# Half of z loaded as bf16 behind v, denser early score pairs, w2 turned by one DMA transpose, and the last output tiles sent one by one

## The chip, the cores and the metric

The kernel runs on one core of one Trainium2 chip. The metric is the device time of one execution in microseconds. "Span" is the profiled execution's time from its first to its last instruction, 2.4 us less than the device time in the kernel before. A time is compared with runs of the kernel before on the same chip, because the chips differ a little.

## The reference

Attention without softmax, gated by u, then a maxout feed-forward layer (8 batches, 3072 rows, 256 columns, z 64 wide, hidden size 1024):

```python
scores = (1.0 / S) * np.matmul(z, z.transpose(0, 2, 1))
attn = np.maximum(scores, 0.0) ** 2
x = (u * np.matmul(attn, v)).reshape(B * S, D)
g = np.maximum(x @ w1, x @ w2)          # computed as relu(x(w1 - w2)) + x w2
out = g @ w_out
```

## The kernel before

The scores are symmetric, so each batch computes only the blocks on and above the diagonal and gets the others by turning them with DMA transposes ("mirrors", tile at_sb). A batch has six groups of 512 rows. Group i runs 48 steps; a step is a pair of matmuls that share the array, one on each half of the rows. Score pairs (two matmuls, two evictions with relu, one square) are made ahead of need, at chosen steps ("slots"), across batch borders. The score matmuls of a batch read zT, the turned z. For batch 0 the opening makes it on TensorE; for batch 1 and later one DMA transpose does it. All DMA transposes and all output stores are issued from the SP queue, in program order; loads that cast from float32 to bf16 are issued from GpSimd's queue.

Names of tiles in the profile lines below: s_ps holds scores as the matmuls leave them in PSUM (the memory that TensorE writes), r_sb the scores after relu, a_sb the squared scores, at_sb their mirrors, zd the doubled z that is turned into zT, acc the sums of a group in PSUM, h_sb these sums after the "drain" (their copy out of PSUM), and un and uT are u before and after its turn.

The parts that matter here (cuts marked by `# ...`):

```python
def pair_slots(i):                       # i counts groups over all batches
    if i == 0: return [1, 3] + list(range(6, 40, 4))
    if i == 1: return list(range(3, 41, 4))
    # ...
V_LATE = [(3, 14), (4, 8), (4, 14), (5, 2), (5, 8), (5, 14)]   # v of batch 1: (group, step)

def ahead(upto):                         # score pairs; some have one half evicted on VectorE
    early = done < 22
    score_pair(*pairs[done], dve_half=1 if early and done % 3 == 0 else None, halves=done == 0)
# ...
# opening: SP loads z of batch 0 in float32 in three pieces (4, 8, 12 tiles); GpSimd's queue
# loads v, then u; GpSimd copies the third piece twice to bf16 (zd); TensorE turns zd into zT
for slot, (n, dc) in enumerate(steps_of(i)):
    ahead(...)                           # emits mirrors too, as blocks become complete
    attn_unit(...)
    # ...
    if later and n % 4 == 0 and (i > 1 or i == 1 and n > 12):
        mirror(*later.pop(0))            # deferred mirrors of groups 0 and 1
    if i == 2 and n == 16:               # w15 = w1 - w2; w2T by 16 TensorE transposes
        # ...
    if (g, n) == (3, 4):                 # zT of the next batch
        double_z(b + 1, 0, NT)           # two VectorE copies
        zT_dma(b + 1)                    # one DMA transpose, SP queue
# after group 2: W2o = w2 w_out from w2T, then the first feed-forward
```

Of the kernel before, what the change touches and what calls it, by code (L numbers as in the profile page):

```python
# [11 lines left out]
def kernel(  # L12
# [10 lines left out]
    nc = tc.nc  # L23
    fp32 = mybir.dt.float32
# [223 lines left out]
    def ff2(b, g, xT, g_sb, last=False):  # L248
        dst = by_tile(out[ds(b * S, S), :])[:, ds(g * G, G), :]
        o_sb = opool.tile([P, G, D], fp32, name="o_sb")  # L250
        for t0 in range(0, G, 2):
            o_ps = mm_psum.tile([P, 2, D], fp32, name="o_ps", tag="mm")
            for t in range(2):
                for dc in range(KD):
                    nc.tensor.matmul(  # L255
                        o_ps[:, t, :],
                        xT[:, dc, ts(t0 + t, P)],
                        W2o_sb[:, dc, :],
                        start=(dc == 0),
                        stop=False,  # L260
                    )
                for nb in range(KF):
                    nc.tensor.matmul(  # L263
                        o_ps[:, t, :],
                        g_sb[:, nb, ts(t0 + t, P)],
                        w_out_sb[:, nb, :],
                        start=False,
                        stop=(nb == KF - 1),
                    )
            nc.scalar.copy(o_sb[:, t0 : t0 + 2, :], o_ps)  # L270
            if last:
                nc.sync.dma_start(out=dst[:, ds(t0, 2), :], in_=o_sb[:, t0 : t0 + 2, :])
        if not last:
            nc.sync.dma_start(out=dst, in_=o_sb)

# [22 lines left out]

    def pair_slots(i):
        if i == 0:  # L300
            return [1, 3] + list(range(6, 40, 4))
        if i == 1:
            return list(range(3, 41, 4))
        if ff_follows(i):
            return [3, 9, 15, 21, 26, 31, 36, 40]
        return [0, 5, 10, 15, 20, 25, 30, 41]
# [39 lines left out]
    with tc.manual_schedule():  # L346
        z32a = first_z(0, 4)
        z32b = first_z(4, 8)
        z32c = first_z(12, 12)
        warm = consts.tile([P, GW], bf16)  # L350
        nc.vector.memset(warm, 0.0)
        load_v(0, 0, G)
        make_identity(nc, ident)
        for g in range(1, NG):
            load_v(0, g * G, G)
        load_u(0, 0)
        load_u(0, 1)
        w1_sb = tpool.tile([P, KD, Dff], bf16, name="w1", tag="at_sb")
        w2_sb = tpool.tile([P, KD, Dff], bf16, name="w2", tag="at_sb")
        w2T_sb = tpool.tile([P, KD, KF, P], bf16, name="w2T", tag="at_sb")  # L360


        def new_acc():
            return {
                (half, dc): acc_psum.tile([P, GW], fp32, name=f"acc{half}{dc}")
                for half in range(2)
                for dc in range(KD)
            }

        first_acc = new_acc()  # L370

        def keep_warm(cols):
            for w in cols:
                nc.tensor.matmul(
                    first_acc[0, 0][:, :w], warm[:, :P], warm[:, :w], start=True, stop=True
                )

        keep_warm([GW] * 5 + [P] * 2)
        double_first(z32a, 0, 4)
        zT_pe(0, 0, 4, "dve")  # L380
        keep_warm([P] * 5)
        double_first(z32b, 4, 4)
        double_first(z32b, 8, 4, at=4)
        on_pool = (nc.gpsimd.tensor_copy, nc.gpsimd.tensor_copy)
        for c in range(0, 12, 4):
            double_first(z32c, 12 + c, 4, at=c, copies=on_pool)
        ahead(1)
        zT_pe(0, 4, 8, "dve")
        keep_warm([P] * 2)
        ahead(2)  # L390
        keep_warm([P] * 4)

        waiting, sums = [], None
        for i, (b, g) in enumerate(groups):
            acc = new_acc() if i else first_acc
            new, slots = {}, pair_slots(i)
            for slot, (n, dc) in enumerate(steps_of(i)):
                k = need[i, n]
                ahead(max(k, min(done + 1, k + AHEAD)) if slot in slots else k)
                if i == 0 and slot in (10, 22):  # L400
                    zT_pe(0, 12 if slot == 10 else 20, 8 if slot == 10 else 4, "act")
                attn_unit(b, g, tiles_of(b, g)[n], acc, dc, n == 0, n == NT - 1)
                if n == NT - 1 and not ff_follows(i):
                    if i < 2:
                        new[dc] = drain_fast(acc, dc)
                    else:
                        new.update(drain(acc, [dc]))
                if dc:
                    continue
                if i in (1, 2) and n == 10:  # L410
                    for h in sums.values():
                        nc.vector.tensor_add(h[0], h[0], h[1])
                    sums = {k: h[0] for k, h in sums.items()}
                if i and n == 12:
                    waiting.append((*groups[i - 1], gate(*groups[i - 1], sums)))
                if i == 0 and n == 14:
                    turn_u(0, 0)
                if i + 1 < len(groups):
                    if i and n == 1:
                        load_u(*groups[i + 1])  # L420
                    if n == 16:
                        turn_u(*groups[i + 1])
                if (i, n) in ((0, 20), (1, 10)):

                    w_in = ((w2_sb, moe_w2), (w1_sb, moe_w1)) if i == 0 else ((w_out_sb, moe_w_out),)
                    nc.vector.memset(w_in[0][0][:, 0, 0:1], 0.0)
                    for w_sb, w in w_in:
                        nc.gpsimd.dma_start(
                            out=w_sb, in_=w.rearrange("(c p) f -> p c f", p=P)
                        )  # L430
                if later and n % 4 == 0 and (i > 1 or i == 1 and n > 12):
                    later.sort(key=lambda block: block[2])
                    mirror(*later.pop(0))
                if i == 2 and n == 16:
                    nc.vector.tensor_sub(w15_sb, w1_sb, w2_sb)
                    for dc in range(KD):
                        tp = mm_psum.tile([P, KF, P], bf16, name="tpw", tag="mm")
                        for j in range(KF):
                            nc.tensor.transpose(
                                tp[:, j, :], w2_sb[:, dc, ts(j, P)], ident  # L440
                            )
                        nc.scalar.copy(w2T_sb[:, dc, :, :], tp)
                if b + 1 < B:
                    late = int(b == 0)
                    if (g, n) == (2, 10 if b else 20):
                        load_z(b + 1, 0, NT, held=late)
                    if (g, n) == (3, 4):
                        double_z(b + 1, 0, NT)
                        zT_dma(b + 1)
                    if g >= 3 and n in (8, 14) and not late:  # L450
                        load_v(b + 1, V_ORDER[2 * (g - 3) + (n == 14)] * G, G)
                    if late and (g, n) in V_LATE:
                        load_v(1, V_ORDER[V_LATE.index((g, n))] * G, G, held=True)
            if i == 2:
                for dc in range(KD):
                    ps = mm_psum.tile([P, D], fp32, name="w2o_ps", tag="mm")
                    for nb in range(KF):
                        nc.tensor.matmul(
                            ps,
                            w2T_sb[:, dc, nb, :],  # L460
                            w_out_sb[:, nb, :],
                            start=(nb == 0),
                            stop=(nb == KF - 1),
                        )
                    nc.scalar.copy(W2o_sb[:, dc, :], ps)

            now = waiting if ff_follows(i) else []
            g_sbs = [ff(w) for w in now[:1]]
            sums = new or drain(acc, range(KD))
            for j, w in enumerate(now):  # L470
                if j:
                    g_sbs.append(ff(w))
                ff2(*w, g_sbs[j])
            if now:
                waiting = []
        w = (*groups[-1], gate(*groups[-1], sums))
        ff2(*w, ff(w), last=True)
# [29 lines left out]
```

## Time and profile before

968.79 us, median of five runs (968.57 to 969.14). What matters:

| what | number |
|---|---|
| TensorE busy | 954.8 of 966.4 us |
| TensorE waits after 60 us | none over 0.2 us |
| first attention matmul / start of group 1 / start of W2o | 7.32 / 23.00 / 52.03 us |
| zT of batch 1: issued / landed / first needed | 74.02 / 80.4 / 86.80 us |

TensorE is the bound: matmuls fill the span but for the opening and the tail. The view of waits of TensorE for the whole span lists who ended its idle time. A line names the engine and the tile that it was about to write, then, behind the arrow, the engine and tile that it waited for, then us in total, times, longest; one wait of 0.2 us is left out:

```profile
PE acc_134 L374 <- DVE warm L351: 1.2, 1, 1.2
PE acc_427 L199 <- DVE a_sb L166: 1.1, 3, 0.5
PE acc_427 L199 <- DVE h_sb L214: 0.5, 1, 0.5
PE s_ps L147 <- DVE r_sb L158: 0.5, 1, 0.5
PE acc_134 L199 <- DMA v_sb<-in_v_dram: 0.4, 1, 0.4
PE s_ps L147 <- ACT zT L105: 0.4, 1, 0.4
PE acc_637 L199 <- DVE a_sb L166: 0.4, 1, 0.4
PE tpz L101 <- ACT zd L88: 0.3, 1, 0.3
```

All of these lie in the first 52 us and sum to 4.8 us. This is the SP queue of the kernel before in order of time (start us, time taken to issue, what):

```profile
34.41 30.73 SPq L181 DMA_TRANSPOSE at_sb<-a_sb  x8
65.24 1.26 SPq L122 DMA_TRANSPOSE uT<-un  x1
66.61 2.13 SPq L181 DMA_TRANSPOSE at_sb<-a_sb  x1
68.83 1.75 SPq L274 DMA_DIRECT2D out_dram<-o_sb  x2
74.02 3.82 SPq L96 DMA_TRANSPOSE zT<-zd  x1
77.94 8.65 SPq L181 DMA_TRANSPOSE at_sb<-a_sb  x2
```

From 34 us on it issues one mirror after the other without a pause, and zT follows the two output stores. The stores' issue ended at 68.83 + 1.75 = 70.58 us; zT waited for its data, the two VectorE copies into zd, until 74.02. The view of tile zd has them (duration min/median/max in ns, first and last start in us; the second ends at 73.4 + 0.55 = 74.0):

```profile
L93 DVE COPY zd<-zn x2: 553/554/554, 73.0 to 73.4; 128x1536 bf16<-128x1536 bf16 x2
```

**So 3.4 us of slack stood ahead of zT.**

### The profile page before, as it was taken

To read this page: it belongs to the slowest core of one execution; us is meant where nothing else is said; L and a number is where in the kernel's file an instruction comes from. 1 tells how busy PE (TensorE), PEld (TensorE's weight loads), DVE (VectorE), ACT (ScalarE), POOL (GpSimd) and SP (SyncE) were. 2 spreads that over 40 slices of the span, in tenths; PEclk is the share of its full clock that TensorE was granted. 3 is DMA by queue.
4 is the path that set the end of the run, shared out by engine and by line. 5 is a ranking of instruction groups with operands and counts; after the bars stand their busy time and mean duration, and the time that the engine had idled before them with its cause. 6 is when DMAs were issued, how large, how long until landed. Compare 5 with 4: busy or idle time off the path is not lost.

```text
span 966.4 us, 19478 instructions
## 1 busy us (share of the span) xinstructions
PE 954.8 (99%) x7994; PEld 621.6 (64%) x8042; DVE 487.2 (50%) x847; ACT 557.6 (58%) x1058; POOL 61.0 (6%) x118
## 2 busy tenths in 40 slices
PE   8999999999999999999999999999999999999998
PEld 4465667675666756667566765676756776566655
DVE  6746454463555534555346553464545554445433
ACT  6757466563575645756456564565556656466433
POOL 3001000100000000000000000000000000000000
PEclk9999999999999999999999999999999999999999
DMA  9999798988689976999869988699967998767611
GB/s 186 186 207 175 135 156 158 179 149 166 134 140 188 146 157 126 164 185 148 150 133 146 184 152 160 131 162 176 150 141 140 157 170 168 135 131 145 124 56 44
DMA packets 382296, 145.99 MB, mean 151 GB/s; under 512 B 360832, under 2 KB 361984, under 8 KB 382208
## 3 DMA queue, kind: packets, MB, share of 16 engines
q1 hardware_dynamic: 365792, 115.25, 62.5%
q0 software_dynamic: 16416, 29.50, 20.8%
q8 instruction: 63, 1.03, 0.4%
q14 instruction: 25, 0.20, 0.1%
HBM read 59.77 MB, written 25.17 MB: 88 GB/s over the span
## 4 chain that ended last, share of the span: by engine, by line
PE 96%; DVE 1%; issue 1%; ACT 1%; DMA 1%; DVEq 0%; POOLq 0%
PE o_ps L263 17%; PE d_ps L234 17%; PE s_ps L147 7%; PE o_ps L255 4%; DMA v_sb<-in_v_dram 1%; DVE a_sb L166 1%; PE acc_12604 L199 1%; PE acc_6354 L199 1%; PE acc_4771 L199 1%; PE acc_3187 L199 1%; PE acc_11103 L199 1%; PE acc_9519 L199 1%; PE acc_7936 L199 1%; PE acc_1582 L199 1%; PE acc_1581 L199 1%
## 5 line engine op out<-in xcount | busy, mean ns | idle before, releaser
L199 PEld LDWEIGHTS <-v_sb 64*128 64x128 bf16 x4608 | 314.6, 94 | 181.4 <-issue 5.9
L160 ACT ACTIVATE r_sb<-s_ps 128x512 bf16<-128x512 f32 (+3 forms) x664 | 333.8, 555 | 90.4 <-PE s_ps L147 88.8
L166 DVE TENSOR_TENSOR a_sb<-r_sb 128x1024 bf16<-128x1024 bf16 x251 | 173.6, 692 | 243.0 <-ACT r_sb L160 239.0
L244 DVE TENSOR_SCALAR g_sb<-d_ps 128x512 bf16<-128x512 f32 x192 | 132.8, 692 | 146.1 <-PE d_ps L234 146.1
L263 PE MATMUL o_ps<-w_out_sb,g_sb 128*128 128x256 bf16 x1536 | 199.1, 273 | 0.0
L234 PE MATMUL d_ps<-xT,w_sb 128*128 128x512 bf16 x720 | 167.4, 379 | 2.6 <-issue 0.2
L263 PEld LDWEIGHTS <-g_sb 128*128 128x128 bf16 x1536 | 150.2, 98 | 20.8
L242 ACT ACTIVATE g_sb<-d_ps 128x512 bf16<-128x512 f32 x192 | 114.8, 598 | 82.0 <-PE d_ps L234 57.1
L147 PE MATMUL s_ps<-zT 64*128 64x512 bf16 (+3 forms) x672 | 148.6, 357 | 0.9 <-DVE r_sb L158 0.5
L270 ACT COPY o_sb<-o_ps 128x512 f32<-128x512 f32 x96 | 56.3, 586 | 150.3 <-PE o_ps L263 149.2
L234 PEld LDWEIGHTS <-w_sb 128*128 128x128 bf16 x768 | 73.2, 98 | 89.6 <-issue 9.8
L255 PE MATMUL o_ps<-W2o_sb,xT 128*128 128x256 bf16 x384 | 73.3, 273 | 0.0
L118 POOL DMA_DIRECT2D un<-in_u_dram x48 | 25.7, 537 | 731.2 <-DMA uT<-un 717.6
L147 PEld LDWEIGHTS <-zT 64*128 64x128 bf16 x672 | 47.6, 94 | 29.0 <-issue 4.6
L220 DVE SCALAR_TENSOR_TENSOR xT<-h_sb,uT 128x512 bf16<-128x512 f32 x96 | 61.8, 685 | 0.0
L164 DVE TENSOR_TENSOR a_sb<-r_sb 128x512 bf16<-128x512 bf16 (+3 forms) x170 | 47.9, 323 | 14.7 <-ACT r_sb L160 14.5
L255 PEld LDWEIGHTS <-xT 128*128 128x128 bf16 x384 | 37.6, 98 | 14.1
L114 POOL DMA_DIRECT2D v_sb<-in_v_dram x48 | 25.8, 546 | 59.1 <-DVE v_sb L113 58.3
L199 PE MATMUL acc_134<-a_sb,v_sb 64*128 64x512 bf16 x24 | 8.7, 377 | 0.5 <-DMA v_sb<-in_v_dram 0.4
L199 PE MATMUL acc_136<-a_sb,v_sb 64*128 64x512 bf16 x24 | 8.7, 378 | 0.0
L199 PE MATMUL acc_137<-a_sb,v_sb 64*128 64x512 bf16 x24 | 8.5, 376 | 0.0
L199 PE MATMUL acc_135<-a_sb,v_sb 64*128 64x512 bf16 x24 | 8.5, 376 | 0.0
(577 smaller groups left out, 1665.3 us busy)
## 6 DMA issues: line engine op xcount, KB each, us to landing
out_dram<-o_sb SPq DMA_DIRECT2D x47, 512.0 KB, 4.0
v_sb<-in_v_dram POOLq DMA_DIRECT2D x48, 256.0 KB, 7.0
un<-in_u_dram POOLq DMA_DIRECT2D x48, 256.0 KB, 5.0
zn<-in_z_dram POOLq DMA_DIRECT2D x7, 384.0 KB, 6.7
a_sb<-a_sb SPq DMA_TRANSPOSE x126, 2.7
at_sb<-a_sb SPq DMA_TRANSPOSE x120, 5.0
uT<-un SPq DMA_TRANSPOSE x48, 3.3
w_132<-in_moe_w_dram POOLq DMA_DIRECT2D x1, 512.0 KB, 5.1
```

The costliest lines, as they stand in the source:

```text
L147: nc.tensor.matmul(s_ps[h][:, lo[h] :], zT[b][rows, 2 * m + h, :], zT[b][rows, g * G + lo[h] // P : g * G + G, :].rearrange("p t c -> p (t ...
L160: nc.scalar.activation(o, s, AF.Relu)
L164: nc.vector.tensor_mul(a[:, k + h, lo[h] :], o, o)
L166: nc.vector.tensor_mul(a[:, k : k + 2, :], r, r)
L199: nc.tensor.matmul(o, v_sb[b][rows, t, ts(dc, P)], mv, start=first, stop=last)
L220: nc.vector.scalar_tensor_tensor(out=xT[:, dc, :].rearrange("p (t r) -> p t r", r=P), in0=hs[dc].rearrange("p (t r) -> p t r", r=P), scala ...
L234: nc.tensor.matmul(d_ps, w15_sb[:, kc, ts(nb, P)], xT[:, kc, :], start=(kc == 0), stop=(kc == KD - 1),)
L242: nc.scalar.activation(g_sb[:, nb, :], d_ps, AF.Relu)
L244: nc.vector.tensor_single_scalar(out=g_sb[:, nb, :], in_=d_ps, scalar=0.0, op=ALU.max)
L255: nc.tensor.matmul(o_ps[:, t, :], xT[:, dc, ts(t0 + t, P)], W2o_sb[:, dc, :], start=(dc == 0), stop=False,)
L263: nc.tensor.matmul(o_ps[:, t, :], g_sb[:, nb, ts(t0 + t, P)], w_out_sb[:, nb, :], start=False, stop=(nb == KF - 1),)
L270: nc.scalar.copy(o_sb[:, t0 : t0 + 2, :], o_ps)
```

## The change

Its intent: (1) take 384 KB of float32 z off the way of the first v block, (2) have more scores ready for groups 0 and 1, (3) free TensorE and ScalarE of the turn of w2, (4) shorten the last copy and store.

```diff
 def ff2(...):
-        for t0 in range(0, G, 2):
-            # two tiles: matmuls, one copy, one store
+        for t0, k in ((0, 2), (2, 1), (3, 1)) if last else ((0, 2), (2, 2)):
+            # k tiles: matmuls, one copy, one store
 # ...
         if i == 0:
-            return [1, 3] + list(range(6, 40, 4))
+            return [1, 3, 6, 9, 12, 15] + list(range(18, 43, 4))
         if i == 1:
-            return list(range(3, 41, 4))
+            return list(range(2, 40, 4))
 # ...
-        z32c = first_z(12, 12)
         load_v(0, 0, G)
-        for g in range(1, NG):
+        load_v(0, G, G)
+        zn[0] = znat.tile([P, NT, dqk], bf16, name="zn")
+        nc.gpsimd.dma_start(out=zn[0][:, 12:, :], in_=by_tile(z[0])[:, 12:, :])
+        for g in range(2, NG):
             load_v(0, g * G, G)
 # ...
-            double_first(z32c, 12 + c, 4, at=c, copies=on_pool)
+            double_first(zn[0], 12 + c, 4, at=12 + c, copies=on_pool)
 # ...
+                if i == 1 and n == 20:
+                    nc.sync.dma_start_transpose(w2T_sb as p (c j) r, w2_sb as p (c f))
                 if i == 2 and n == 16:
                     nc.vector.tensor_sub(w15_sb, w1_sb, w2_sb)
-                    # 16 TensorE transposes and 2 ScalarE copies into w2T_sb
```

More of the change, by code (lines that the diff above doesn't have):

```diff
@@ L250, in ff2 @@
         o_sb = opool.tile([P, G, D], fp32, name="o_sb")
-        for t0 in range(0, G, 2):
-            o_ps = mm_psum.tile([P, 2, D], fp32, name="o_ps", tag="mm")
-            for t in range(2):
+        for t0, k in ((0, 2), (2, 1), (3, 1)) if last else ((0, 2), (2, 2)):
+            o_ps = mm_psum.tile([P, k, D], fp32, name="o_ps", tag="mm")
+            for t in range(k):
                 for dc in range(KD):
@@ L269, in ff2 @@
                     )
-            nc.scalar.copy(o_sb[:, t0 : t0 + 2, :], o_ps)
+            nc.scalar.copy(o_sb[:, t0 : t0 + k, :], o_ps)
             if last:
-                nc.sync.dma_start(out=dst[:, ds(t0, 2), :], in_=o_sb[:, t0 : t0 + 2, :])
+                nc.sync.dma_start(out=dst[:, ds(t0, k), :], in_=o_sb[:, t0 : t0 + k, :])
         if not last:
@@ L433 @@
                     mirror(*later.pop(0))
+                if i == 1 and n == 20:
+                    nc.sync.dma_start_transpose(
+                        w2T_sb.rearrange("p c j r -> p (c j) r"),
+                        w2_sb.rearrange("p c f -> p (c f)"),
+                    )
                 if i == 2 and n == 16:
                     nc.vector.tensor_sub(w15_sb, w1_sb, w2_sb)
-                    for dc in range(KD):
-                        tp = mm_psum.tile([P, KF, P], bf16, name="tpw", tag="mm")
-                        for j in range(KF):
-                            nc.tensor.transpose(
-                                tp[:, j, :], w2_sb[:, dc, ts(j, P)], ident
-                            )
-                        nc.scalar.copy(w2T_sb[:, dc, :, :], tp)
                 if b + 1 < B:
```

## The prediction

> **What bounds the kernel.** TensorE. The page gives PE 954.8 us busy of 966.4 (99%), and the table of stages shows 837.6 of 840 us between 100 and 940 us. The change cannot touch that. What is left is the opening (0 to 52 us) and the tail (after the last matmul, about 962.4 us). A unit pair of attention matmuls starts every 0.215 us, a score pair takes another 0.215. Counting slots, group 0 (7.3 to 23.0 us) has about 2.2 us of TensorE holes, group 1 (to 38.2) about 2.7, group 2 (to 52.0) about 0.6. The timeline shows their causes: in group 0 a score pair waits for the zT copy on ScalarE (12.88) and the next group for the drain on VectorE (23.00); in group 1 matmuls wait for squared scores made just in time (32.06, 32.85, 34.66, 36.66).
>
> **1. z by a bf16 cast load behind v.** Its 384 KB float32 load leaves the SP queue. Loads of all queues run on the same 16 DMA engines (the Trainium skill, "Trainium Kernel Development and Optimization", Key Constraints; the DMA row at 4 to 8 us agrees, both queues sharing 16 busy engines), so v block 0 should land near 5.6 instead of 7.3 us. The first attention matmul waited only 0.43 us for it, and the next score pair waits at 7.59 us for VectorE's zT copy anyway: gain under 0.2 us. The z half should land near 8 us (before: 7.5). GpSimd's casts (0.40 us, some 0.86) then finish the first eight tiles at about 10.2 us, and their transposes run at 10.9: no wait expected.
>
> **2. Denser score slots.** Group 0 gets 13 pairs instead of 11. ScalarE needs 1.08 us for a pair (two 0.55 us evictions), more than the 0.86 us that three steps and a score take, and it is full from 8 to 12.8 us already. So group 0 gets longer: the pair at slot 12 comes two steps after the transposes and waits about 1.0 us instead of 0.5; a second zT copy costs about 0.4; the pair at slot 42 puts two evictions and a square (0.69 us) ahead of the drain, so group 1 starts near 24.7 us instead of 23.0. Group 1 has two more pairs ready (lead of 18 steps instead of 9) and should lose most of its holes: end near 37.9 (before 38.18). Two pairs (0.43 us) are moved from later.
>
> **3. w2 by one DMA transpose.** Removes 16 PE transposes (TensorE 46.6 to 47.7 us: 1.1 us) and two ScalarE copies (1.01 us each), and with them the hole at 51.06. Adds one transpose like an at_sb mirror (landing 5 to 7 us) to the SP queue in a stretch where the DMA engines are full; I expect landing near 49.5 us, W2o starting near 50.3 us (before 52.03). A wait there of up to 1 us is possible.
>
> **4. Tail.** Last copy 128x256 instead of 128x512 (0.37 against 0.59 us) and half the last store: 0.4 us.
>
> **Sum.** Opening 2.0, tail 0.4: 2.4 us, all on the critical path. Predicted 966.4 us, range 963.8 to 968.4. Faster by over 2%: 0.005; within 2%: 0.985; slower: 0.01.
>
> **Right or wrong shows in:** first v landing near 5.6 us and first attention matmul near 7.0; a wait of about 1 us for the zT copy near 12.9; group 1 starting later, not earlier; almost no waits for a_sb in group 1; W2o start 50 to 50.6 us without a wait for w2T; end of last matmul to end of span 3.5 us (before 3.9).
>
> **What would make it wrong.** The z half queuing behind more of v, so that the zT transposes wait for GpSimd; the drain at the first group's end costing more than estimated; w2T landing late or pushing mirrors into group 3.

## The result

979.42 us, median of five runs, **from 972.95 to 982.69**: 1.0102 times the kernel before (interval 1.0064 to 1.0140). Ratios here and below are the mean time of one kernel's runs over that of the other's of the same rounds, so not quite the ratio of the medians quoted. The prediction of 966.4 us (963.8 to 968.4) was wrong, and in the wrong direction: the class "within 2%" held, but a gain of 2.4 us was a loss of 10.6. The changed kernel also scatters over 9.7 us, the kernel before over 0.6 (later the changed kernel over 4.3, the kernel before over up to 3.5).

The same view of TensorE's waits, changed kernel:

```profile
PE s_ps L147 <- DMA zT<-zd: 10.2, 1, 10.2
PE s_ps L147 <- DVE r_sb L158: 1.2, 1, 1.2
PE acc_444 L199 <- DVE h_sb L214: 1.2, 1, 1.2
...
PE tpz L101 <- POOL zd L88: 1.1, 1, 1.1
PE s_ps L147 <- ACT zT L105: 0.6, 1, 0.6
```

One wait is new and as large as the whole loss: a score pair waits **10.2 us for the DMA transpose that turns z into zT**. The waits for a_sb, which the denser slots were to remove, are gone; in the opening those for r_sb and h_sb grew from 0.5 to 1.2 us each, that for the zT copy from 0.4 to 0.6, and one for GpSimd of 1.1 us is new. The instructions on tile zT between 50 and 130 us in the kernel before (the DMA transpose: min/median/max of the time to issue in ns, first and last start in us; the last line is issue to landing):

```profile
L96 SPq DMA_TRANSPOSE zT<-zd x1: 3822/3822/3822, 74.0 to 74.0; - x1
...
DMA to landing us min/median/max: 6.4/6.4/6.4
```

The same view of the changed kernel:

```profile
L96 SPq DMA_TRANSPOSE zT<-zd x1: 4435/4435/4435, 78.6 to 78.6; - x1
...
DMA to landing us min/median/max: 15.4/15.4/15.4
```

zT was issued 4.6 us later (78.6, before 74.0) and took 15.4 us to land (before 6.4). It landed at 94.0 (before 80.4). Its data were no later than before:

```profile
L93 DVE COPY zd<-zn x2: 554/555/556, 72.9 to 73.4; 128x1536 bf16<-128x1536 bf16 x2
```

So it was the queue that held it. The SP queue of the changed kernel shows why:

```profile
46.14 3.51 SPq L438 DMA_TRANSPOSE w2T<-w_132  x1
49.70 21.61 SPq L181 DMA_TRANSPOSE at_sb<-a_sb  x7
71.40 1.73 SPq L122 DMA_TRANSPOSE uT<-un  x1
73.22 1.01 SPq L275 DMA_DIRECT2D out_dram<-o_sb  x2
74.33 4.21 SPq L181 DMA_TRANSPOSE at_sb<-a_sb  x1
78.63 4.43 SPq L96 DMA_TRANSPOSE zT<-zd  x1
```

The w2T transpose took 3.51 us of the queue. Everything behind it moved back: the same nine mirrors (two of them ahead of w2T here) and the stores ended at 74.23 instead of 70.58 us, so the slack of 3.4 us was gone. Then a mirror that stood behind zT before stands ahead of it (74.33, 4.21 us to issue), because two more score pairs are done by then and one of them completed its block. A third thing is the need: the 43rd score pair, the first of batch 1, ran at 86.80 us before and is asked for at 83.9 us now.

The long landing shows in the DMA view, but its cause does not. GpSimd's queue issues the casting loads of v and u of batch 1 at 79.00, 79.52 and 84.75 us in the changed kernel (79.06, 79.58, 84.81 before). Before, zT had nearly landed when they came; now they fall on it. The two DMA queues between 84 and 88 us, when both queues are active in both kernels. Columns: packets, MB, share of 16 engines' time; q1 carries the transposes, q0 the casting loads. Kernel before:

```profile
q1 hardware_dynamic: 2051, 0.52, 67.2%
q0 software_dynamic: 177, 0.30, 49.0%
```

The changed kernel, same view and stretch:

```profile
q1 hardware_dynamic: 986, 0.25, 89.9%
q0 software_dynamic: 102, 0.19, 41.4%
```

In those 4 us the transposes moved 0.25 MB instead of 0.52, at a greater share of the engines: 0.899 x 16 x 4 us / 986 = 58 ns for a packet, against 0.672 x 16 x 4 us / 2051 = 21 ns. (The shares of the two queues sum to over 100%, so packets overlap in time.) That the casting loads slow the packets is not shown by this: in the same stretch of the kernel before they ran beside transposes too, at 21 ns.

Last, the table of stages of the changed kernel (length, busy time by engine, granted clock, DMA share, GB/s):

```profile
83.50:94.00 10.50, 0.38 (x4) 0.00 (x0) 0.70 (x2) 0.21 (x1) 0.53 (x1) 0.70 1.29 111
94.00:98.00 4.00, 3.93 (x21) 2.46 (x23) 0.84 (x3) 1.50 (x4) 0.00 (x0) 0.51 1.23 207
98.00:104.00 6.00, 6.00 (x59) 5.23 (x56) 3.53 (x8) 4.12 (x9) 0.78 (x2) 1.00 0.52 108
```

After the wait the TensorE clock is granted at 0.51 for 4 us, so about 4.0 x 0.49 = 2.0 us more is lost. The Trainium skill, "TensorE: Matmul & The Clock Gate" (What's actually happening), says that an idle window of about 3.4 us halves the clock and about 3.4 us of sustained work restores it; this trace agrees (the clock halved at 87.7 us, 3.8 us after TensorE ran dry at 83.9, and was full again 3.9 us after work resumed at 94.07). Other runs below fit less well: a wait of 2.8 us (e4) already halved the clock, one of 2.1 us (e3) did not, and in r1 it was full only 5.9 us after work resumed.

The sum closes: +10.2 (wait) +2.0 (half clock) -0.4 (two pairs ahead, 0.215 us each) -0.1 (W2o at 51.97, before 52.03) -0.5 (tail) = 11.2 us, and the span grew by 11.2 (966.4 to 977.6).

### The profile page after: what moved, and what is told of

The parts are those of the page before. It is cut to its first block, busy times and chain, and to the rows that moved or that the text cites. A ratio compares the mean times of both kernels' runs of the same rounds, so it can differ in the third digit from the quotient of the medians. Undisturbed runs are those within 1.5% of the kernel's fastest.

```text
span 977.6 us, 19445 instructions
## 1 busy us (share of the span) xinstructions
PE 955.7 (98%) x7978; PEld 624.1 (64%) x8026; DVE 487.3 (50%) x847; ACT 555.7 (57%) x1057; POOL 61.9 (6%) x119
## 4 chain that ended last, share of the span: by engine, by line
PE 95%; DMA 2%; issue 1%; DVE 1%; ACT 0%; POOL 0%; POOLq 0%
PE o_ps L264 17%; PE d_ps L234 17%; PE s_ps L147 7%; PE o_ps L256 4%; DMA zT<-zd 2%; PE acc_12585 L199 1%; PE acc_4752 L199 1%; PE acc_6335 L199 1%; PE acc_1581 L199 1%; PE acc_11083 L199 1%; PE acc_9501 L199 1%; PE acc_9500 L199 1%; PE acc_7917 L199 1%; PE acc_3169 L199 1%; PE acc_11084 L199 1%
## 5 line engine op out<-in xcount | busy, mean ns | idle before, releaser
L147 PE MATMUL s_ps<-zT 64*128 64x512 bf16 (+3 forms) x672 | 150.0, 359 | 12.2 <-DMA zT<-zd 10.2
L271 ACT COPY o_sb<-o_ps 128x512 f32<-128x512 f32 (+1 forms) x97 | 56.3, 581 | 150.0 <-PE o_ps L264 148.9
L164 DVE TENSOR_TENSOR a_sb<-r_sb 128x512 bf16<-128x512 bf16 (+3 forms) x170 | 47.9, 323 | 27.0 <-ACT r_sb L160 26.8
```

The source lines that it names most:

```text
L147: nc.tensor.matmul(s_ps[h][:, lo[h] :], zT[b][rows, 2 * m + h, :], zT[b][rows, g * G + lo[h] // P : g * G + G, :].rearrange("p t c -> p (t ...
L164: nc.vector.tensor_mul(a[:, k + h, lo[h] :], o, o)
L271: nc.scalar.copy(o_sb[:, t0 : t0 + k, :], o_ps)
```

## The experiments

**Theory.** w2T and one mirror ahead of zT in the SP queue, and the earlier need, make zT late; then it meets the casting loads and lands later still (the second half is not settled, see e4). **Rivals.** The denser slots alone do it; or w2T alone; or the z load behind v has a part; or the long landing has a cause of its own. There were sixteen runs: thirteen new kernels, two of them twice (r2 repeats e8, b3_again repeats b3), and the changed kernel once more (r1). All gave the right result.

| kernel | parts of the change | median (us) | ratio to before (95%) | wait for zT in the profile |
|---|---|---|---|---|
| changed | all four | 979.42 | 1.0102 (1.0064 to 1.0140) | 10.2 |
| e1_w2_on_pe | all but w2T | 968.43 | 1.0008 (0.9988 to 1.0029) | none |
| e2_old_slots | all but slots | 968.76 | 0.9997 (0.9982 to 1.0012) | none |
| e3_zt_first | all, zT ahead of the mirror | 969.42 | 1.0017 (0.9989 to 1.0045) | 2.1 |
| e4_v_later | all, v loads later | 971.93 | 1.0029 (1.0014 to 1.0044) | 2.8 |
| e5_only_z | z load alone | 968.86 | 0.9998 (0.9982 to 1.0013) | none |
| e6_only_slots | slots alone | 968.34 | 0.9992 (0.9976 to 1.0009) | none |
| e7_only_w2 | w2T alone | 970.32 | 1.0009 (0.9985 to 1.0034) | none |
| b1_mended | slots, w2T, tail; zT first, v later | 968.56 | 0.9991 (0.9976 to 1.0006) | 1.7 |
| e8_slots_w2 | slots and w2T | 973.06 | 1.0042 (1.0025 to 1.0059) | 3.3 |
| e9_only_tail | tail alone | 968.05 | 0.9987 (0.9970 to 1.0004) | none |
| b2_w2_in_the_gap | candidate | 971.82 | 1.0019 (0.9990 to 1.0049) | none |
| b3_w2_on_pe | candidate | 966.99 | 0.9978 (0.9963 to 0.9993) | 0.3 |
| r1_changed_again | all four | 975.50 | 1.0067 (1.0054 to 1.0080) | 6.3 |
| r2_slots_w2_again | slots and w2T | 975.92 | 1.0066 (1.0054 to 1.0079) | 3.5, and 3.6 in later batches |
| e10_zt_first_v_later | all, zT first, v later | 969.23 | 1.0006 (0.9993 to 1.0019) | 0.5 |
| b3_again | candidate | 966.01 | 0.9969 (0.9957 to 0.9981) | 0.3 |

The kernel before ran between 968.31 and 971.85 us (e1 to e4: median 968.83; e5 to b1: 969.45; e8 to b3: 969.62; the last four: 969.23). e5 to b1 and e8 to b3 ran on one chip, and the median for e8 to b3 is of the same seven runs of the kernel before and one more.

### One part taken away: e1 and e2

e1 puts the 16 TensorE transposes and two copies of w2 back; e2 puts the old slots back.

```diff
-                if i == 1 and n == 20:
-                    nc.sync.dma_start_transpose(w2T ...)          # e1
+                    # i == 2 and n == 16: 16 TensorE transposes, 2 ScalarE copies
```
```diff
-            return [1, 3, 6, 9, 12, 15] + list(range(18, 43, 4))  # e2
+            return [1, 3] + list(range(6, 40, 4))
-            return list(range(2, 40, 4))
+            return list(range(3, 41, 4))
```

> The changed kernel with w2 turned by the 16 TensorE transposes again, all else kept. Theory (the turn of z for batch 1 is late because two more transposes stand ahead of it in the SP queue, w2T 3.5 us and one mirror 4.2 us, and it then falls in with the casting loads of v and u): the out stores leave near 70.6 us, zT is issued near 74 instead of 78.6 us, lands near 81 (before 80.4) instead of 94.0, TensorE waits under 1 us for it (changed kernel 10.2), granted clock 1.0 throughout, time 967 to 970 us. Rival (the denser score slots alone ask for zT of batch 1 too early, at 83.7 instead of about 87 us, so the wait stays without w2T): a wait for zT of over 5 us, time 975 to 980.

> The changed kernel with the score slots of before, all else kept. Theory: zT stands behind w2T but ahead of the extra mirror, is issued near 74.5 us and lands near 81; batch 1 is asked for near 86 us; no wait for zT; time 966.5 to 968.5. Rival (w2T alone makes zT late): zT issued after 77 us, a wait of over 3 us, time over 973.

Either removal ended the wait in the profile and the loss in the median. The view of tile zT in e1:

```profile
L96 SPq DMA_TRANSPOSE zT<-zd x1: 4346/4346/4346, 75.7 to 75.7; - x1
...
DMA to landing us min/median/max: 7.4/7.4/7.4
```

And in e2:

```profile
L96 SPq DMA_TRANSPOSE zT<-zd x1: 4937/4937/4937, 73.9 to 73.9; - x1
...
DMA to landing us min/median/max: 8.5/8.5/8.5
```

In e1 it is issued at 75.7 and lands at 83.1 us (near 74 and 81 expected); in e2 at 73.9 and 82.4. Each removal alone lets zT land before TensorE asks for it. With w2T but without the extra mirror zT is issued no later than before (73.9, before 74.0: the stores' issue ended at 73.38); with the mirror but without w2T it comes 1.7 us later (1.0 in e6 below); only both together make it 4.6 us. Both rivals that name one part alone fall. e2 missed in one thing: it waited 1.7 us for a mirror (at_sb), so w2T held up a mirror instead; that wait is larger than the 1.1 us of TensorE time that w2T frees. One of e1's four runs took 972.18 us at a granted clock of 0.996, so some scatter stays without w2T.

### One cause taken away with all parts kept: e3, e4 and e10

e3 moves the two VectorE copies into zd along with the turn (65.8 instead of 72.9 us).

```diff
+            if i == 3:                       # e3 and e10: at the head of group 3
+                double_z(1, 0, NT)
+                zT_dma(1)
-                    if (g, n) == (3, 4):
+                    if (g, n) == (3, 4) and b:
```
```diff
-    V_LATE = [(3, 14), (4, 8), (4, 14), (5, 2), (5, 8), (5, 14)]   # e4 and e10
+    V_LATE = [(4, 14), (4, 18), (4, 22), (5, 2), (5, 8), (5, 14)]
```

> The changed kernel with the doubling and turn of z of batch 1 emitted at the head of group 3, so that only the one mirror no longer stands ahead of zT in the SP queue. Theory: zT issued near 74.3 us, lands by 82, before it is asked for at 83.7: no wait, clock 1.0, time 966 to 968 us (the changed kernel less 10.2 us of wait and about 2 us of half clock). Rival (the landing of 15.4 us has another cause than the casting loads that begin at 79.0 us): lands 10 us or more after its issue, TensorE waits, time over 970.

> The changed kernel with the casting loads of v of batch 1 held back by 14 or more steps (the first begins in group 4 at step 14, not in group 3), so zT stays late in the queue but meets no v load. Theory (half of the damage is the meeting): zT issued near 78 to 80 us, lands 6 to 8 us later, near 86, TensorE waits 1 to 3 us instead of 10.2, time 968 to 971 us. Rival (queue order alone): landing still over 12 us after issue, wait over 7 us, time over 975.

> All four parts of the change, with the turn of z of batch 1 at the head of group 3 and the v loads of batch 1 held back. Theory (late issue and the meeting with casting loads account for all of the loss): wait for zT under 2 us, no run over 971, median 967 to 969, within 1 us of the kernel before. Rival (something else of the change costs too): median over 970.

e3 moved the issue to 75.0 us; the wait fell from 10.2 to 2.1 us, not to nothing, since the landing still took 10.9 us beside the loads from 79 us on. It missed the time expected (969.42, I had said 966 to 968), and two marks of the rival came true: a landing of over 10 us and a wait. e4 left zT late (78.0) but took the v loads away from it: the landing took 8.4 us and the wait 2.8; its time (971.93) is outside the 968 to 971 expected. Against the first profile the wait fell by 7.4 us in e4 (10.2 to 2.8) and by 8.1 in e3 (10.2 to 2.1), together more than the wait itself, so the two would not be independent. But the comparison is weak: the unaltered kernel did not run in this call, in its repetition (r1, below) the landing took 10.9 us and the wait was 6.3, and e8, with the v loads in place, landed in 9.2 us. e3 is within noise of the kernel before on its chip (1.0017) and e4 is not (1.0029), so the place in the queue is shown to matter; **the share of the casting loads is argued, not shown.** One of e3's runs took 974.76 us. e10 does both; no run of it was over 970.63, and its profile shows 0.5 us of wait and a granted clock of 0.999:

```profile
PE acc L199 <- DVE h_sb L214: 1.4, 2, 1.2
PE s_ps L147 <- DVE r_sb L158: 1.2, 1, 1.2
...
PE s_ps L147 <- DMA zT<-zd: 0.5, 1, 0.5
```

e10 is level with the kernel before (1.0006), while the unaltered changed kernel on the same chip was at 1.0067 (r1). So zT's lateness accounts for the loss; which of the two mends did how much, e10 can't tell. It is not faster: the wins of the change are small, see below. Its landing still took 9.9 us, 3.5 us more than before, though the u load at 74.46 us is the only casting load near it; in these 9.9 us the transposes' queue also moved the output stores (1.99 MB, in the 6.4 us before 0.94). So casting loads of v are not needed for a landing of 10 us.

### One part alone: e5, e6, e7, e9

Each is the kernel before with one part of the diff above and nothing else.

> The kernel before with the bf16 load of half of z behind v, nothing else changed. The prediction's view: this part costs nothing (z half lands near 8 us, GpSimd's first four copies done by 10.2, transposes at 10.9), W2o starts at 52.0 us as before, time 968.6 to 968.9. Theory after the result: z half lands near 9.8 us, the transposes wait about 1 us for GpSimd, W2o starts 0.6 to 1.2 us later than 52.03, time 969.3 to 970.2.

> The kernel before with the denser score slots, nothing else changed. The prediction's view: group 1 starts near 24.7 us but has almost no holes after, W2o starts near 51.4 us, time about 967. Theory after the result: the drain waits 1.2 us at the first group's end, and a score pair of group 1 waits 1.2 us for VectorE, so W2o starts between 51.8 and 52.3 us with two pairs more done; zT stands behind one more mirror only, no wait for it over 0.5 us; time 968.0 to 968.8.

> The kernel before with w2 turned by one DMA transpose, nothing else changed. The prediction's view: W2o starts near 50.6 us, 1.4 us earlier, and all of it is kept: time 967.2 to 967.6. Theory after the result: W2o starts near 50.7 us, but the SP queue runs 3 to 4 us later and a mirror or zT is waited for in groups 3 to 5 by 0 to 2 us, different from run to run; time 967.5 to 969.5 with more scatter than the 0.7 us of before.

> The kernel before with the last output tiles leaving one by one, nothing else changed. The prediction's view, which the changed kernel's trace supports: from the last matmul's end to the span's end 3.5 us instead of 4.0, time 968.2 to 968.6, 0.3 to 0.6 under the kernel before of the same call.

e5 (z behind v): no measurable difference (the interval is 1.5 us wide to either side), which the prediction had and my later theory had not. The profile shows a trade: the wait for the first v block is gone, and a wait for GpSimd has come (0.4 us here, 1.1 in the changed kernel). GpSimd's copies of z began at 9.3 us instead of 7.5, and the six of them took 3.48 us from bf16, before 3.04 us from float32.

e6 (slots): 968.34, and group 1 shorter by only 0.8 us (24.61 to 39.02, before 23.00 to 38.18; predicted 24.7 to 37.9). The prediction was right about group 0 and wrong about group 1. TensorE's timeline of e6, the two rows with a wait between 24 and 37 us (start, duration, what; in brackets the idle time before it and who ended it):

```profile
24.61 0.61 PE L199 MATMUL acc<-at_sb,v_sb 64*128 64x512 bf16 x4 [1.20 <-DVE h_sb L214]
...
35.25 0.37 PE L147 MATMUL s_ps<-zT 64*128 64x512 bf16 x1 [1.20 <-DVE r_sb L158]
```

VectorE in e6 at that time (start, duration, what):

```profile
31.50 1.29 DVE L412 TENSOR_TENSOR h_sb<-h_sb 128x512 f32<-128x512 f32 x2
...
33.31 1.29 DVE L220 SCALAR_TENSOR_TENSOR xT<-h_sb,uT 128x512 bf16<-128x512 f32 x2
34.52 0.68 DVE L158 TENSOR_SCALAR r_sb<-s_ps 128x512 bf16<-128x512 f32 x1
```

The relu half that VectorE does for the 22nd pair stands behind the adds and gates of the finished group (31.50 to 34.6 us). It holds a PSUM buffer, so the score pair that needs the buffer stops TensorE until 35.25. Two pairs of lead don't help against that; four waits for a_sb (1.5 us in all) went, and the wait for r_sb, 0.5 us before, became 1.2.

e7 (w2T): TensorE is freed of the transposes, and group 1's start (23.95) to W2o (51.99) takes 28.04 us, before 29.03: a gain of 1.0 us (predicted: the transposes' 1.1 and a hole of 0.4). It did not arrive: the median is 970.32 (967.5 to 969.5 expected) with runs at 967.75, 968.37, 972.26 and 972.37. In the profiled run, one of the fast ones, the first v block came late (a wait of 1.6 us, before 0.4), which used the gain up. It shows no late wait, so where the slow ones lose 4 us is open.

e9 (tail): from the start of the last copy to the end of the span 3.35 us (962.75 to 966.1), before 3.95 (962.45 to 966.4). The times lean the same way (968.05, 969.62 for the kernel before on that chip), but the interval includes 1.

### Two parts: e8, and e8 and the changed kernel on one chip

e8 is the changed kernel without the z load and the tail. It lost 0.42% (973.06). The time was as expected, the profile less bad than that: zT issued at 76.5 (77 or later expected), landing 9.2 us (over 10), wait 3.3 us (over 4). The loss was less than the changed kernel's, so both were run again on one chip (r1, r2).

> The kernel before with the denser slots and the DMA transpose of w2 together, but with the load of z and the tail of before. Theory (these two parts together, and no other, make zT of batch 1 late: w2T and one more mirror ahead of it, and casting loads from 79 us on): zT issued at 77 us or later, landing over 10 us, TensorE waits over 4 us, granted clock under 1.0 in the whole span, time 973 to 982. Rival (the z load behind v is needed for it too): wait under 2 us, time 967 to 970.

> The changed kernel again, unaltered, for its scatter and beside the next. Theory: 972 to 983 us, a wait for zT of 4 us or more in the profile, transposes' packets three times as long while they share the engines with casting loads. If the first set was a chip's peculiarity: 973 or less in most runs.

> The denser slots and the DMA transpose of w2 without the z load and the tail, again, on the same chip as the changed kernel. If the z load behind v has no part in the loss: within 1 us of the changed kernel plus the tail's 0.5. If it has (it shifts the opening by 1 us and zT's issue further into the v load): 3 us or more under it, near 973.

On one chip they are equal, 1.0067 and 1.0066. So **slots and w2T together are enough for the whole loss, and the z load and the tail have no measurable part in it** (the intervals leave some 1.7 us open). The first results differed because of the chip, of scatter, or both. zT of r1:

```profile
L96 SPq DMA_TRANSPOSE zT<-zd x1: 6842/6842/6842, 78.5 to 78.5; - x1
...
DMA to landing us min/median/max: 10.9/10.9/10.9
```

The issue is late as in the first profile (78.5, 78.6; e8 and r2: 76.5 and 76.2) but the landing took 10.9 us, not 15.4, and the wait was 6.3 us. So the queue's delay is steady and the landing is what varies, between 9.2 and 15.4 us in the profiles of the changed kernel, r1, e8 and r2. r2 waited only 3.5 us here and another 3.6 us for zT of later batches, which no other profile shows, so its equal time is made up differently. My expectation of packets three times as long failed: between 80 and 84 us, where r1's transposes shared the engines with casting loads, a packet took 20 ns. (It was 50 ns between 76 and 80 us, but there larger packets of the output stores are mixed in.) During the 15.4 us of the first landing all queues together moved 1.87 MB, 121 GB/s; during r1's 10.9 us they moved 2.04 MB, 187 GB/s, more of it casting loads (0.79 against 0.66 MB). So the first profile's longest landing comes from a lower rate of all queues and not from more casting bytes. What lowers the rate is open.

### Candidates: b1, b2, b3

> The changed kernel with the opening load of z as before (float32, SP queue), the turn of z of batch 1 emitted at the head of group 3, and the v loads of batch 1 held back to group 4 step 14 and later. Theory: no wait for zT (issued near 74, lands by 82, asked for at 83 or later), no wait for GpSimd near 11 us, clock 1.0; against before it keeps two score pairs (0.43 us), the transposes' 1.1 us less the two 1.2 us waits and the tail of 0.5: time 965.5 to 967.5. Rival (late mirrors then hold it up): a wait for at_sb over 1 us, time 968 or more.

> A candidate: w2 loaded ahead of the other weights and turned by DMA in group 0, where the SP queue stood idle from 22 to 28 us; z load as before; no score pair in the last eight steps of group 0; no VectorE half for the pair that held a PSUM buffer; turn of z of batch 1 at the head of group 3; tail as changed. Theory: w2T issued between 20 and 24 us, group 1 starts near 23.7, W2o near 49.5, zT issued near 71 and landed by 78, no wait over 1 us after 25 us: time 964 to 966. Rival (the transposes of this stretch are limited by the engines that move them, not by the queue's order): mirrors or w2T are waited for by 2 us or more, time 968 or more.

> The same candidate with w2 turned on TensorE as before. Theory: zT issued near 70.5, no wait for it; W2o near 50.6 us; time 965.5 to 967.

> The candidate with w2 turned on TensorE, z load as before, the mended slots, the turn of z of batch 1 at the head of group 3 and the new tail, on another chip: 0.1 to 0.3% faster than the kernel before, median 966 to 968. If the first result came from the noisier runs of before in that call: no difference.

b1 keeps w2T on DMA with both mends: no gain (968.56, expected 965.5 to 967.5), zT landed after 9.9 us and was waited for by 1.7. b2 loads and turns w2 earlier, where the SP queue had stood idle; but the u load then came later, the uT transposes took the gap (20.1 to 26.8 us), w2T left at 27.06 instead of 22, and three of four runs took over 971 us (964 to 966 expected). Why they did isn't shown: the profiled one is the fast one. b3 gives up w2T and keeps what worked:

```diff
 # against the kernel before
+        (tail as in the change)
         if i == 0:
-            return [1, 3] + list(range(6, 40, 4))
+            return [1, 3, 6, 9, 12, 15] + list(range(18, 39, 4))   # none in the last steps
         if i == 1:
-            return list(range(3, 41, 4))
+            return list(range(2, 40, 4))
-            early = done < 22
+            early = done < 20                # the 22nd pair leaves VectorE alone
+            if i == 3:                       # zT of batch 1 at the head of group 3
+                double_z(1, 0, NT)
+                zT_dma(1)
```

Its waits of TensorE, second run (left out: the one of 1.2 us for tile warm at the start, and one of 0.2):

```profile
PE acc L199 <- DVE h_sb L214: 0.8, 2, 0.4
PE acc L199 <- DMA v_sb<-in_v_dram: 0.6, 1, 0.6
PE s_ps L147 <- ACT zT L105: 0.6, 1, 0.6
PE s_ps L147 <- DMA zT<-zd: 0.3, 1, 0.3
```

The 1.2 us waits for the drain and for r_sb are gone, W2o starts at 50.37 us, and the time is **966.01 us, 0.31% under the kernel before (0.9969, interval 0.9957 to 0.9981)**, and 0.22% in the other call. It beats the kernel before on two chips, and the changed kernel on the one where both ran (0.9969 against 1.0067). Which of its parts gives the 0.3% was not tested one by one.

## Why the prediction was wrong

- **The step that failed is the costing of step 3.** I wrote that w2T "adds one transpose like an at_sb mirror ... to the SP queue in a stretch where the DMA engines are full", asked only when w2T itself would land, and put its whole cost down as "a wait there of up to 1 us". w2T was never waited for. The transfers behind it in the same queue paid: it took 3.51 us of a queue that had 3.4 us of slack ahead of zT. Alone that was just absorbed (zT issued at 73.9 in e2 and 74.0 in e7, as before), but nothing was left for the mirror of step 2, and zT went out at 78.6 and was waited for by 10.2 us (6.3 in r1). That slack can be read in the SP queue's timeline of the kernel before; the prediction made no use of it. "Pushing mirrors into group 3" stood among the doubts, but the transfer that mattered was zT of batch 1, which I had not followed.
- **Steps 2 and 3 were costed apart.** Each alone is within noise of before (e1, e2, e6, e7), though two of e7's four runs lost 4 us in a way that no profile shows. Together they put two more transposes ahead of zT, asked for it 2.9 us sooner, and let it overlap the casting loads, whose share is not settled. The sum "2.0 + 0.4, all on the critical path" has no such term, and it was +12.2 us with the half clock.
- **Opening, mis-sized.** Predicted gain at W2o 1.7 us plus two pairs; the first profile had 0.1, other profiles of the same opening up to 1.2 (e10, W2o at 50.86). Two terms were missing: VectorE's relu half in group 1 (1.2 us; I had group 1 end near 37.9, it ended at 39.8; the kernel before had this wait already, 0.5 us at 32.06, and I had counted it among the waits for squared scores, which more lead removes) and, in some runs, GpSimd (0.2 to 1.2 us; I had "no wait expected"). The z half landed at 9.9 us, not 8.
- **Right:** no measurable gain of the z load (e5, which can't resolve the 0.2 us); group 1 starting later; no waits for a_sb left in group 1; 1.0 us of TensorE time from w2T by the time of W2o (e7); the tail, 3.41 us from the last copy's start to the end (before 3.95; predicted 3.5 from the last matmul's end). The first v block landed at 6.2 us (predicted 5.6) and the first attention matmul ran at 6.77 (predicted 7.0). The wait for the zT copy was 0.56, not 1.0 us.
- **The range was too narrow.** A width of 4.6 us suits a kernel that scatters over 0.6 us; the changed kernel scattered over 9.7 us (4.3 in r1, where the kernel before scattered over 2.8).

Open: why a late zT takes 9 to 15 us to land, from run to run, and what share the casting loads have in it; where the slow runs of e7 and b2 lose their time.

## What to carry to other kernels

When work is moved to a DMA queue, look for the first transfer behind it in that queue that an engine will wait for, and measure the queue's idle time ahead of that transfer; the moved transfer's own deadline is the lesser question. Changes that make things earlier (more pairs ahead) also reorder a shared queue and move deadlines forward, so cost two such changes together. A stall of TensorE can cost more than itself: here waits of 2.8 to 10.2 us were followed by work at half clock that lost another 1.4 to 3.0 us (e4, e8, the changed kernel, r2, r1; half of the time worked at half clock), and a wait of 2.1 us (e3) lost nothing more.

## What the Trainium skill lacked or had wrong

- "Advanced Engine Details and Errata" (X-Bar Transpose) says that transpose DMAs are as fast as regular ones. Here transposes with nothing beside them moved 215 GB/s between 68 and 70 us and 288 GB/s between 42 and 44 us in the kernel before, with the engines full, and the last output store about 400 GB/s at its height. And no page gives the rate of transposes beside other transfers: one and the same transpose (128 x 24 x 128 bf16, 768 KB) took 6.4 us from issue to landing in the kernel before and 15.4 us in the changed one.
- "DMA: Bandwidth & Descriptors" (Queues, rings and completion order) says that an engine takes turns between queues by the packet. That fits small transpose packets (0.25 MB / 986 = 250 bytes) losing to casting packets (0.19 MB / 102 = 1.9 KB), but the same mixture ran at 21 ns a packet in the kernel before and at 20 ns in r1 (58 in the changed kernel's first profile), so it doesn't explain the difference; what does is open.
- "TensorE: Matmul & The Clock Gate" (Part 4: PE-mode transpose) gives about 275 ns for a transpose in a kernel's context. Here 16 of them took 1.07 us from first to last (219 ns each, overlapped, 57 ns apart), which makes the turn of w2 on TensorE much cheaper than that figure suggests.
- No page says how much the time varies for which issuing one DMA transpose occupies the SP queue: mirrors of one shape took 1.80 to 6.40 us in the first 120 us of the kernel before. What sets it was not tested.
